# Holding the early loads of a fused linear-attention and SwiGLU kernel, and another split of its last output tile

## The chip, the core and the metric

The kernel runs on one core of a Trainium2 chip. The metric is the device time of one execution in microseconds (us). The core has a matrix engine (TensorE, in the profile PE, with PEld for its weight loads), a vector engine (VectorE, DVE), a scalar engine (ScalarE, ACT), a general engine (GpSimd, POOL) and a sequencer that issues DMAs (SyncE, SP). Each engine works through its own list of instructions in order, and waits on semaphores for the others.

## The reference

The input x has 2048 tokens of 640 numbers in bfloat16. It is normalised once, and two branches are added to it:

```python
xn = _layernorm(x)                                   # 2048 x 640
q, k, v = split(xn @ wqkv)                           # 32 heads of 20
pq, pk  = q @ w_phi, k @ w_phi                       # per head, 20 x 20
phi_q   = concat(softmax(pq), softmax(-pq))          # 40 features; phi_k alike
kv, z   = phi_k^T v, sum of phi_k over the tokens
A       = (phi_q kv / (phi_q z + 1e-6)) @ wo
B       = (silu(xn @ w1) * (xn @ w3)) @ w2           # inner width 1536
out     = x + A + B
```

## The kernel before

**A planner.** The kernel describes its work as operations with the memory that each reads and writes, and a list scheduler in `_Program.schedule` orders them at build time: it keeps a clock for each engine with assumed durations, and takes the ready operation that could start first, among near equals the one with the higher level (a due time turned round). Up to 175 us of its clock the width of "near equal" is drawn from a random generator started with `SEED`. `emit` then writes the order out for each engine with the semaphore waits that the dependencies need. A DMA that depends on another DMA makes SP wait for that one's landing. Nearly all instructions are recorded by two helpers, so PE's matmuls have the line L619, the other engines' L627, plain DMAs L689 and DMA transposes L693.

**Units on PE.** A unit is a chain of matmuls into one, two or four of the eight PSUM banks. Its name says what it computes:
- V4, K4: value and feature-mapped key projection of token tile 4 (16 tiles of 128 tokens), 10 matmuls of 320 columns each. K's weights are wk folded with w_phi (the "fold" units, which read the transposed wk or wq and write `Wkp` or `Wqp`). ScalarE takes the exponentials of K's result into `ekt`, VectorE sums them over each head (the TENSOR_REDUCE) and inverts the sum, GpSimd multiplies.
- M0.3: the MLP's gate and up product for block 0 (512 tokens) and chunk 3 of 12 of the inner width, 10 matmuls of 512 columns. ScalarE computes a tanh into `th`, VectorE two steps `t` and `hT`, and then the banks are free.
- Q0.1: the feature-mapped query of a block, 5 matmuls of 512 columns and two exponentials.
- kv_sum, kv_back: the sum over all tokens and its way back into the layout that the queries need.
- qt4: query times kv for tile 4, always in banks 4 to 7; ScalarE copies the denominators, VectorE divides and writes the product. The next qt can start when the product is written.
- O15: the output of tile 15, 12 chunks of hT by w2 and 5 of oT by wo, 640 columns in two banks; VectorE adds x, SP stores.

**Tokens and transposes.** x is loaded with tokens on the partitions (`x_tok`: tiles 0 to 3 one by one, tiles 4-7, 8-11 and 12-15 as loads of 640 KB). VectorE computes statistics, GpSimd the inverse deviation, VectorE or ScalarE normalises in place. Tiles 0 to 3 are transposed on PE; each tile from 4 on by one DMA transpose from SP (`turn`, here "turn 4" for tile 4) into `xnT`, which V, K, M and Q read.

**The early loads.** All go out on SP, but for four at the start on ScalarE's queue. Their order follows their levels. After x's first tiles, wv, the first third of w1 and w3 (480 KB each) and w_phi come the five transposes of wk. Then, in order of level: x tiles 4-7, w1 and w3 (second third, columns 384 to 768), x tiles 8-11, w1 and w3 (768 to 1152), x tiles 12-15, w1 and w3 (1152 to 1536), five transposes of wq. In the kernel before each of these waits for the last transpose of wk (`d.raw.add(o)`, in the list from `P.all[n]` on) and for nothing else, so SP issues them one after another.

**The last output tile.** O15 is computed in two halves of 320 columns, each with its own bank, addition and store, so that the first half's tail runs beside the second half's matmuls.

Of the kernel before, what the change touches and what calls it, by code (L numbers as in the profile page):

```python
# [5 lines left out]
ALU = mybir.AluOpType  # L6
# [4 lines left out]
D = 640  # L11
# [3 lines left out]
T = S // 128  # L15
# [477 lines left out]
CENTRED = {0: "ACT", 1: "ACT", 2: "ACT", 3: "DVE"}  # L493
POOLED = ()
TURNED = ()
SEED = 65
TRIPLES = ((0, 3, 0, 60), (3, 3, 60, 60), (6, 3, 120, 60), (9, 3, 180, 60), (12, 3, 240, 60), (13, 3, 300, 20))


def bass_parallel_sum__linear_kernel_hedgehog__glu_gated_swiglu__prompt_kernel(  # L500
# [13 lines left out]
    P = _Program(nc)  # L514
# [12 lines left out]
    def new(name, shape, dtype, offset=None):  # L527
        size = mybir.dt.size(dtype)
        for n in shape[1:]:
            size *= n  # L530
        return P.sbuf(name, shape, dtype, region(size) if offset is None else offset)
# [23 lines left out]
    xres = new("xres", [128, 4, D], bf)  # L555
# [42 lines left out]
    def bank(k, cols=512, off=0, p0=0, p1=128):  # L598
        return PS[p0:p1, k * 512 + off:k * 512 + off + cols]

    def bank2(k, cols):
        return PS[:, k * 512:(k + 2) * 512].rearrange("p (b c) -> p b c", c=512)[:, :, 0:cols]

    def free(ap):
        n = 1
        for s in ap.shape[1:]:
            n *= s
        return n
# [6 lines left out]
    def mm(j, o, l, r, start, stop, shared=False, busy=None):  # L615
        u, n = P.unit, free(r)

        def emit():
            return nc.tensor.matmul(o(u.k), l, r, start=start, stop=stop, skip_group_check=shared)  # L619
        return P.mm(emit, [l, r], j, max(n / 2400 + 0.0025, 0.035) if busy is None else busy, n)  # L620

    def way(eng, name, args, kw, busy, lat):
        u = P.unit
        e = {"ACT": nc.scalar, "DVE": nc.vector, "POOL": nc.gpsimd}[eng]

        def emit():
            return getattr(e, name)(*[at(a, u) for a in args], **{k: at(v, u) for k, v in kw.items()})  # L627
        emit.__name__ = name
        return eng, (emit, busy, lat)
# [5 lines left out]
    def sb(*aps):  # L635
        return [a for a in aps if hasattr(a, "ap")]

    def add(ways, w, r, banks=None, level=0.0, after=(), part=False):
        o = P.op(dict(ways), sb(*w), sb(*r), banks, level, after)
        o.part = part  # L640
        return o
# [11 lines left out]
    def w_tt(eng, o, a, b, f, n, fast=1):  # L653
        if eng == "DVE":
            return way(eng, "tensor_tensor", (o, a, b, f), {}, 0.07 + n / 960 / fast, 0.15 + n / 960 / fast)
        return way(eng, "tensor_tensor", (o, a, b, f), {}, 0.14 + n * 1.7 / 1000, 0.18 + n * 1.7 / 1000)
# [25 lines left out]
    def pieces(o, elem):  # L682
        n = 1
        for s in o.shape:
            n *= s
        return n * 2 / elem / 16, max(18.5, 12 + 0.04 * elem) / 1e3

    def load(o, i, level=0.0, eng="SP", after=()):
        return P.dma(eng, lambda: queue[eng].dma_start(o, i), sb(o), sb(i), *pieces(o, 2 * o.shape[-1]), 0.45, level,  # L689
                     after)  # L690

    def turn(o, i, level=0.0, dram=False, after=()):
        d = P.dma("SP", lambda: nc.sync.dma_start_transpose(o, i), sb(o), sb(i), *pieces(o, 256),  # L693
                  1.31, level, after)
        d.extra = 1.0 if dram else 0.2
        return d
# [4 lines left out]
    out_t = out.rearrange("b (t p) d -> p (b t) d", p=128)  # L701
# [5 lines left out]
    def load_x(a, b, level, eng="SP", after=()):  # L707
        return load(x_tok[:, a:b, :], x_t[:, a:b, :], level, eng, after)

    def load_w1(a, b, level, eng="SP"):  # L710
        return load(w1_s[:, :, a:b], w1_t[:, :, a:b], level, eng)

    def load_w3(a, b, level, eng="SP"):
        return load(w3_s[:, :, a:b], w3_t[:, :, a:b], level, eng)

    def load_w13(a, b, level, eng="SP"):
        load_w1(a, b, level, eng)
        load_w3(a, b, level, eng)

    def load_wT(which, e, level, after=()):  # L720
        return turn(wqkT[:, which * DC + e:which * DC + e + 1, :],
                    A_wqkv[:, which * D + 128 * e:which * D + 128 * e + 128], level, True, after)
# [42 lines left out]
    def ln_stats(t0, n, level):  # L765
        for t in range(t0, t0 + n):
            for q in range(2):
                i, o = x_tok[:, t, 320 * q:320 * q + 320], bst[:, t, 6 * q:6 * q + 6]
                add([w_op("DVE", "bn_stats", (o, i), 0.48, 0.5)], [o], [i], None, level)
            o, i = mv[:, t, 0:2], bst[:, t, 0:12]  # L770
            add([w_op("DVE", "bn_aggr", (o, i), 0.13, 0.21)], [o], [i], None, level)
        m, v, r, z = mv[:, t0:t0 + n, 0], mv[:, t0:t0 + n, 1], mv[:, t0:t0 + n, 4], mv[:, t0:t0 + n, 6]
        add([w_op("POOL", "tensor_scalar_add", (r, v, EPS), 0.21, 0.25)], [r], [v], None, level)
        add([w_op("POOL", "tensor_tensor", (r, r, mhalf[:, 0:n], ALU.pow), 0.55 + 0.1 * (n - 1),
                  0.6 + 0.1 * (n - 1))], [r], [r, mhalf[:, 0:n]], None, level)
        if t0 >= 4:
            add([w_op("POOL", "tensor_scalar_mul", (z, m, -1.0), 0.21, 0.25)], [z], [m], None, level)
            add([w_op("POOL", "tensor_tensor", (z, z, r, ALU.mult), 0.21, 0.25)], [z], [z, r], None, level)

    def ln_apply(t, level):  # L780
        o, m, s, z = x_tok[:, t, :], mv[:, t, 0:1], mv[:, t, 4:5], mv[:, t, 6:7]
        ways = [w_op("DVE", "tensor_scalar", (o, o, m, s, ALU.subtract, ALU.mult), 0.35, 0.44)]
        if t in POOLED:
            ways = [w_op("POOL", "tensor_scalar", (o, o, m, s, ALU.subtract, ALU.mult), 2.5, 2.55)]
        if t >= 4:
            ways.append(w_act(o, o, ACT.Identity, D, s, z))
        add(ways, [o], [o, m, s, z] if t >= 4 else [o, m, s], None, level)
# [274 lines left out]
    finish = []  # L1062

    def out_tile(t, level):
        b, ti = divmod(t, 4)
        u = P.begin(2, level, stream="O")
        u.name = f"O{t}"
        chunks = [(hT[b][:, i, ti * 128:(ti + 1) * 128], w2_s, i) for i in range(FC)]
        chunks += [(oT[:, i, t * 128:(t + 1) * 128], wo_s, i) for i in range(DC)]
        r = xres[:, t % 4, :].rearrange("p (b c) -> p b c", c=320)  # L1070
        load(xres[:, t % 4, :], x_t[:, t, :], 2e5 - 2 * t)
        if t < 4:
            P.all[-1].early = 60.0
        last = t == T - 1
        for qs in ([(0,), (1,)] if last else [(0, 1)]):
            for n, (l, w, i) in enumerate(chunks):
                for q in qs:
                    mm(q, lambda k, q=q: bank(k + q, 320), l, w[:, i, 320 * q:320 * q + 320], n == 0,
                       n == len(chunks) - 1)
            if last:  # L1080
                q = qs[0]
                add([w_tt("DVE", r[:, q, :], lambda k, q=q: bank(k + q, 320), r[:, q, :], ALU.add, 320)],
                    [r[:, q, :]], [r[:, q, :]], [q], 2e6)
                finish.append(load(out_t[:, t, 320 * q:320 * q + 320], r[:, q, :], 3e5))
            else:
                if qs[0] == 0:
                    add([w_tt("DVE", r, lambda k: bank2(k, 320), r, ALU.add, D)], [xres[:, t % 4, :]],
                        [xres[:, t % 4, :]], [0, 1], 1e6)
                    finish.append(load(out_t[:, t, :], xres[:, t % 4, :], 3e5 - 2 * t))

    def filler(t, until):
        u = P.begin(1, 0.0)
# [36 lines left out]
    for e in range(DC):  # L1129
        o = load_wT(1, e, lv - 9 - e, first)  # L1130
    load_x(4, 8, lv - 19, "SP", [o])
    n = len(P.all)
    load_w13(384, 768, lv - 20)
    load_x(8, 12, lv - 21)
    load_w13(768, 1152, lv - 22)
    load_x(12, 16, lv - 23)
    load_w13(1152, 1536, lv - 24)
    for e in range(DC):
        load_wT(0, e, lv - 30 - e)
    for d in P.all[n:]:  # L1140
        d.raw.add(o)

    up = 2e6
    for t in range(4):
# [2 lines left out]
    n = len(P.all)  # L1147
# [13 lines left out]
    for t in range(4, T, 2):  # L1161
        ln_stats(t, 2, 1e5 - t)
        ln_apply(t, 2e5 - t)
        ln_apply(t + 1, 2e5 - t)
        turn(xnT[:, :, t * 128:(t + 1) * 128], x_tok[:, t, :], lv)
        turn(xnT[:, :, t * 128 + 128:(t + 2) * 128], x_tok[:, t + 1, :], lv)

    def when(us):
        return 1000.0 - us
# [11 lines left out]
    n = len(P.all)  # L1181
# [8 lines left out]
    for b in range(3):  # L1190
        for fc in range(FC):
            n = 12 * b + fc
# [6 lines left out]
    for b in range(NB):  # L1199
        for j in range(4):  # L1200
            t = 4 * b + j
# [6 lines left out]

    P.schedule({"PE": 1.25, "ACT": 1.12, "DVE": 0.93, "POOL": 0.8, "SP": 0.81}, filler, 12.0, SEED, 175.0)

# [60 lines left out]
```

The softmax here doesn't subtract the row's maximum and nothing guards it: scores larger than these inputs give would overflow.

## Time and profile before

| | us |
|---|---|
| median of 4 runs | 276.12 (275.6 to 277.5) |
| the profiled execution | 277.5 |
| its span, first to last instruction | 275.7 |
| PE busy | 269.6 (98%) |
| VectorE busy | 183.6 (67%) |
| ScalarE busy | 102.7 (37%) |
| GpSimd busy | 60.4 (22%) |

The granted PE clock is 1.000. The runs are 277.5, 276.15, 275.6 and 276.1; the profiled execution is the first of them. Times inside the profile count from the span's start. In a timeline row the columns are the start, the length, the engine, the line, the operation with what it writes and reads, the count, and in brackets how long the engine stood idle before it and whose event came last before it went on. Merged rows count several instructions. A DMA row of the issues has size and the time from issue to landing. A "q" after an engine's name means its sequencer: the length of an SPq row is the time that issuing took.

### The profile page before, as it was taken

To read this page: it belongs to the slowest core of one execution; us is meant where nothing else is said; L and a number is where in the kernel's file an instruction comes from. 1 tells how busy PE (TensorE), PEld (TensorE's weight loads), DVE (VectorE), ACT (ScalarE), POOL (GpSimd) and SP (SyncE) were. 2 spreads that over 40 slices of the span, in tenths; PEclk is the share of its full clock that TensorE was granted. 3 is DMA by queue.
4 is the path that set the end of the run, shared out by engine and by line. 5 is a ranking of instruction groups with operands and counts; after the bars stand their busy time and mean duration, and the time that the engine had idled before them with its cause. 6 is when DMAs were issued, how large, how long until landed. Compare 5 with 4: busy or idle time off the path is not lost.

```text
span 275.7 us, 5081 instructions
## 1 busy us (share of the span) xinstructions
PE 269.6 (98%) x2104; PEld 159.8 (58%) x2104; DVE 183.6 (67%) x322; ACT 102.7 (37%) x188; POOL 60.4 (22%) x101
## 2 busy tenths in 40 slices
PE   8999979999999999999999999999999999999996
PEld 4747447765664446544444445777677774444774
DVE  5848886999999544478769986277677215566212
ACT  5637628874455441237383364010110002322000
POOL 4500633699989800000000000000000000000000
PEclk9999999999999999999999999999999999999999
DMA  7569998771000000802131111234343322000001
GB/s 234 153 95 283 342 158 174 121 207 57 0 0 2 0 0 2 270 18 26 24 50 21 27 26 25 72 95 85 98 110 80 90 71 74 0 0 0 26 24 48
DMA packets 41287, 21.98 MB, mean 80 GB/s; under 512 B 27056, under 2 KB 41264, under 8 KB 41264
## 3 DMA queue, kind: packets, MB, share of 16 engines
q1 hardware_dynamic: 40688, 21.01, 31.7%
q10 hardware_dynamic: 576, 0.66, 0.7%
q8 instruction: 16, 0.26, 0.4%
q14 instruction: 7, 0.06, 0.1%
HBM read 12.81 MB, written 2.62 MB: 56 GB/s over the span
## 4 chain that ended last, share of the span: by engine, by line
PE 93%; DMA 2%; DVE 2%; issue 1%; ACT 0%; ACTq 0%; DVEq 0%
PE PS L619 92%; DMA x_tok<-in_A_x_dram 2%; DVE bst L627 0%; PE PS L857 0%; DVE t L627 0%; DVE hT L627 0%; ACTq L689 0%; DVE Wqp L627 0%; ACT th L627 0%; ACT L627 0%; DVE xres L627 0%; DVE rS L627 0%; DVE xc L627 0%; DVE x_tok L627 0%; PE PS L1099 0%
## 5 line engine op out<-in xcount | busy, mean ns | idle before, releaser
L619 PE MATMUL PS<-xnT,w_s 128*128 128x512 bf16 x480 | 107.3, 379 | 0.0
L619 PEld LDWEIGHTS PS<-xnT,w_s 128*128 128x128 bf16 x480 | 46.4, 98 | 54.1 <-DVE hT L627 0.3
L619 PE MATMUL PS<-w_s,hT 128*128 128x320 bf16 x384 | 55.0, 299 | 0.0
L627 ACT ACTIVATE th<-PS 128x512 f32<-128x512 f32 x48 | 28.7, 598 | 64.0 <-PE PS L619 63.8
L627 DVE SCALAR_TENSOR_TENSOR t<-th,PS 128x512 bf16<-128x512 f32 x48 | 32.8, 683 | 26.4 <-ACT th L627 26.3
L619 PEld LDWEIGHTS PS<-w_s,hT 128*128 128x128 bf16 x384 | 37.0, 98 | 14.9
L627 POOL TENSOR_TENSOR ekt<-ekt,rS 128x640 bf16<-128x640 bf16 x32 | 39.6, 1276 | 1.9 <-DVE rS L627 1.9
L627 DVE TENSOR_TENSOR xres<-PS,xres 128x640 bf16<-128x640 f32 (+1 forms) x17 | 13.4, 785 | 39.0 <-PE PS L619 39.0
L627 DVE SCALAR_TENSOR_TENSOR hT<-t,PS 128x512 bf16<-128x512 bf16 x48 | 32.6, 678 | 1.3 <-DVE t L627 0.2
L627 ACT ACTIVATE EqT<-PS 128x512 bf16<-128x512 f32 x40 | 21.9, 594 | 12.0 <-PE PS L619 12.0
L627 ACT ACTIVATE e_s<-PS 128x64 f32<-128x64 f32 x32 | 9.1, 283 | 44.3 <-PE PS L619 43.9
L619 PE MATMUL PS<-wo_s,oT 128*128 128x320 bf16 x160 | 24.5, 299 | 0.0
L627 DVE TENSOR_TENSOR prod<-PS,g_s 128x1280 bf16<-128x1280 f32 x16 | 23.9, 1491 | 0.5
L619 PE MATMUL PS<-Wkp,xnT 128*128 128x320 bf16 x160 | 23.9, 299 | 0.0
L627 ACT ACTIVATE ekt<-PS 128x640 bf16<-128x640 f32 x32 | 20.8, 700 | 7.7 <-PE PS L619 7.5
L619 PE MATMUL PS<-xnT,Wqp 128*128 128x512 bf16 x100 | 23.4, 380 | 0.0
L627 DVE TENSOR_REDUCE S<-ekt 128x64 f32<-128x1280 bf16 x16 | 22.8, 1449 | 0.0
L619 PE MATMUL PS<-wv,xnT 128*128 128x320 bf16 x120 | 18.3, 299 | 1.7 <-DVE bst L627 1.7
L619 PEld LDWEIGHTS PS<-wo_s,oT 128*128 128x128 bf16 x160 | 15.7, 98 | 6.1
L619 PEld LDWEIGHTS PS<-Wkp,xnT 128*128 128x128 bf16 x160 | 15.5, 98 | 6.1 <-ACT Wkp L627 0.2
L627 DVE BATCH_NORM_STATS2 bst<-x_tok 128x6 f32<-128x320 bf16 x32 | 14.2, 471 | 3.8 <-DMA x_tok<-in_A_x_dram 3.8
L619 PEld LDWEIGHTS PS<-wv,xnT 128*128 128x128 bf16 x120 | 11.7, 98 | 7.3 <-DVE bst L627 2.2
(69 smaller groups left out, 168.1 us busy)
## 6 DMA issues: line engine op xcount, KB each, us to landing
w_s<-in_B_w_dram SPq DMA_DIRECT2D x8, 480.0 KB, 7.5
xres<-in_A_x_dram SPq DMA_DIRECT2D x16, 160.0 KB, 2.2
out_dram<-xres SPq DMA_DIRECT2D x15, 160.0 KB, 1.8
x_tok<-in_A_x_dram SPq DMA_DIRECT2D x3, 640.0 KB, 7.5
w_s<-in_B_w_dram SPq DMA_DIRECT2D x1, 1920.0 KB, 9.0
wo_s<-in_A_wo_dram SPq DMA_DIRECT2D x1, 800.0 KB, 5.6
x_tok<-in_A_x_dram SPq DMA_DIRECT2D x2, 160.0 KB, 3.6
x_tok<-in_A_x_dram ACTq DMA_DIRECT2D x2, 160.0 KB, 4.4
```

Source lines behind the costliest of these rows:

```text
L619: return nc.tensor.matmul(o(u.k), l, r, start=start, stop=stop, skip_group_check=shared)
L627: return getattr(e, name)(*[at(a, u) for a in args], **{k: at(v, u) for k, v in kw.items()})
```

## The change

Three things change.
- The list of loads that wait for the last transpose of wk is replaced by a chain: each load from the fourth on (counted from x tiles 4-7) waits for the landing of the third before it, so that at most three are on the way. x tiles 4-7 and the second third of w1 wait for the transpose of wk as before; the second third of w3, third in the list, waits for nothing now. x tiles 8-11 wait besides for `held`'s added dependency, the DMA transpose of tile 5 (which SP issues after that of tile 4).
- The last output tile is split into 384 and 256 columns.
- The planner's random generator starts from another number, so that the order of units, and of the work on all engines, differs in many places up to its 175 us, and behind.

```diff
-SEED = 65
+SEED = 136
...
-        last = t == T - 1
-        for qs in ([(0,), (1,)] if last else [(0, 1)]):
...
+        for q, c0, c1 in ((0, 0, 384), (1, 384, D)):
+            for n, (l, w, i) in enumerate(chunks):
+                mm(q, lambda k, q=q, c=c1 - c0: bank(k + q, c), l, w[:, i, c0:c1], n == 0, n == len(chunks) - 1)
+            o = xres[:, t % 4, c0:c1]
+            add([w_tt("DVE", o, lambda k, q=q, c=c1 - c0: bank(k + q, c), o, ALU.add, c1 - c0)], [o], [o], [q], 2e6)
+            finish.append(load(out_t[:, t, c0:c1], o, 3e5))
...
-    n = len(P.all)
+    n = len(P.all) - 1
     load_w13(384, 768, lv - 20)
     load_x(8, 12, lv - 21)
+    held = P.all[-1]
     load_w13(768, 1152, lv - 22)
     load_x(12, 16, lv - 23)
     load_w13(1152, 1536, lv - 24)
     for e in range(DC):
         load_wT(0, e, lv - 30 - e)
-    for d in P.all[n:]:
-        d.raw.add(o)
+    for m in range(n + 3, len(P.all)):
+        P.all[m].raw.add(P.all[m - 3])
+    P.all[n + 1].raw.add(o)
...
         turn(xnT[:, :, t * 128:(t + 1) * 128], x_tok[:, t, :], lv)
         turn(xnT[:, :, t * 128 + 128:(t + 2) * 128], x_tok[:, t + 1, :], lv)
+        if t == 4:
+            held.raw.add(P.all[-1])
```

In the order that the planner makes of the changed program, SP's list from w_phi on reads: w3 (384 to 768), five wk transposes, w3 (768 to 1152), x tiles 4-7, w1 (384 to 768), w3 (1152 to 1536), w1 (768 to 1152), one wq transpose, turns 4 and 5, w1 (1152 to 1536), turns 6 and 7, x tiles 8-11, a wq transpose, x tiles 12-15, two wq transposes, turns 8 to 11, the last wq transpose, turns 12 to 15. PE's list from the folds of wk on reads: K0 to K3, M0.3, M0.4, M0.5, V4, K4 and so on to K7, M0.6, M0.7, V8, K8 and so on to V12 with the folds of wq, where the kernel before has M0.6 ahead of V4 and M0.7 ahead of V12.

More of the change, by code (lines that the diff above doesn't have):

```diff
@@ L1073, in out_tile @@
             P.all[-1].early = 60.0
-        last = t == T - 1
-        for qs in ([(0,), (1,)] if last else [(0, 1)]):
+        if t < T - 1:
             for n, (l, w, i) in enumerate(chunks):
-                for q in qs:
+                for q in range(2):
                     mm(q, lambda k, q=q: bank(k + q, 320), l, w[:, i, 320 * q:320 * q + 320], n == 0,
                        n == len(chunks) - 1)
[L1080 to L1089, printed above, removed]
+            add([w_tt("DVE", r, lambda k: bank2(k, 320), r, ALU.add, D)], [xres[:, t % 4, :]],
+                [xres[:, t % 4, :]], [0, 1], 1e6)
+            finish.append(load(out_t[:, t, :], xres[:, t % 4, :], 3e5 - 2 * t))
+            return
+        for q, c0, c1 in ((0, 0, 384), (1, 384, D)):
[4 more added lines that the diff above has]
+            finish.append(load(out_t[:, t, c0:c1], o, 3e5))
     def filler(t, until):
```

## The prediction

> **What bounds the kernel now.** I read the page's busy shares and slices first, then TensorE's (PE's) timeline for its idle places, then the DMA landings around them.
>
> ```profile
> span 275.7 us, 5081 instructions
> PE 269.6 (98%) x2104; PEld 159.8 (58%) x2104; DVE 183.6 (67%) x322; ACT 102.7 (37%) x188; POOL 60.4 (22%) x101
> PE   8999979999999999999999999999999999999996
> ```
>
> PE works 98% of the span at full clock, in an order fixed when the program is built. The change does not alter PE's amount of work, so only PE's 6.1 us of idle time can be won. The sixth slice (a 7) is the one hole between start and end. PE's timeline gives its place:
>
> ```profile
> 28.36 8.80 PE L619 MATMUL PS<-xnT,w_s 128*128 128x512 bf16 x40
> 38.89 1.52 PE L619 MATMUL PS<-wv,xnT 128*128 128x320 bf16 x10 [1.74 <-DVE bst L627]
> 40.25 1.52 PE L619 MATMUL PS<-Wkp,xnT 128*128 128x320 bf16 x10
> 64.45 1.52 PE L619 MATMUL PS<-Wkp,xnT 128*128 128x320 bf16 x10
> 66.22 0.80 PE L619 MATMUL PS<-BDc,wqkT 128*128 128x140 bf16 x12 [0.25 <-DVE Wqp L627]
> ```
>
> Ten matmuls of 512 columns start 2.157 us before their successor (60.62 to 62.78), ten of 320 columns 1.358 (38.89 to 40.25 and on). So four MLP units (M0.3 to M0.6) from 28.36 would end at 36.99; V4, the value projection of token tile 4, starts at 38.89: 1.90 us lost. In the same way 64.45 + 1.36 = 65.81 against 66.22: 0.41 us lost at a fold of wq. Everything later stands nose to tail.
>
> The name in the first bracket is not the cause: the statistics that VectorE computes there are of tiles 8 on, and V4 does not read them. V4 needs the transpose of tile 4 (turn 4). From SP's timeline and the DMA issues, its issue and landing, and those of some loads before it:
>
> ```profile
> 28.86 3.06 SPq L693 DMA_TRANSPOSE xnT<-x_tok  x1
> xnT<-x_tok SPq DMA_TRANSPOSE x1, 9.9
> ...
> x_tok<-in_A_x_dram SPq DMA_DIRECT2D x1, 640.0 KB, 4.2
> ...
> w_s<-in_B_w_dram SPq DMA_DIRECT2D x1, 480.0 KB, 5.3
> ...
> w_s<-in_B_w_dram SPq DMA_DIRECT2D x1, 480.0 KB, 8.5
> ...
> xnT<-x_tok SPq DMA_TRANSPOSE x1, 2.7
> ```
>
> Turn 4 is issued at 28.86 and lands 9.9 us later, at 38.76; a transpose with nothing queued takes 2.7 (the last row, issued at 44.32). The difference is the queue: the loads issued from 20.28 land 4.2, 5.3, 6.3, 7.5, 8.5, 8.5, 10.3 and 10.1 us after their issue, that is at 24.5, 26.0, 27.6, 29.3, 30.9, 32.3, 35.7 and 37.0. Turn 4 stands behind all of them.
>
> **The change, part by part**, from the instruction order of the changed program.
>
> *What moves on SP.* The second third of w3 goes out at 4.3, ahead of the wk transposes, and the last-but-one w3 piece right behind them at 18.4. The DMA engines are idle from about 10 to 12.6 and from 19.7 to 21.3 in the trace; a 480 KB load takes 1.5 (32.3 - 30.9) to 1.6, so both fit. Both bounds for what they cost: nothing if they stay in the holes, or 0.3 us for the wk transposes (the last lands 20.2; the fold at 21.01 needs it by 21.28, 1.0 us of cover). I take nothing.
>
> Token tiles 4-7 go out at 20.28 as before and land at 24.5; w1's second piece lands at 26.0; the next w3 piece waits for a landing at 18.4 + 4.3 = 22.7 and takes third place, landing 27.5. Then come one w1 piece (issued 26.0) and one wq transpose (SP 27.5 to 28.8). Behind them are turns 4 and 5 at 28.86 (statistics and normalising on VectorE keep their order, ended 28.8 before) and 30.2. Ahead of turn 4 in the queue are then one w1 piece, sent by 28.1, and one transpose. Landing: 2.7 (alone) to 4.4 (a transpose from HBM, issued behind a load at 39.03), so 31.6 to 33.3.
>
> *What moves on PE.* M0.6 goes behind K7, so V4 is reached at 28.36 + 3 x 2.157 = 34.83. Turn 4 is there 1.5 to 3.2 earlier; turns 5, 6, 7 (issued 30.2, 33.3, 34.6, after 2.7 to 4.4) are needed at 37.55, 40.27 and 42.98 and have at least 2.5. V4's PSUM banks come from M0.4: on VectorE a sum over heads ends at 32.4 (31.0 + 1.4), then M0.3's hT, M0.4's t and hT follow at 0.6 to 0.7 each, so 34.3: 0.5 to spare. So the 1.90 us go; from V4 on every unit runs 1.90 earlier for the same work done.
>
> *The added waits.* SP stops for landings, and what stands behind is held too. Tiles 8-11 wait for turn 5, but SP comes to them only at 35.9 (after turns 6 and 7); landing 4.2 later, 40.1. Tiles 12-15 wait for that landing: 40.2 + 4.2 = 44.4. A wq transpose waits for it (44.4 to 45.7), and turns 8 to 11 stand behind at 45.7, 47.0, 48.3 and 49.6. Turn 8 lands at 48.4. PE needs it after eight projections (10.87) and two MLP units (4.31): 34.83 + 15.18 = 50.0. Cover 1.6 us. Turn 12, issued at 53.2 after its normalising, lands by 57.6, needed at 60.9. The remaining wq transposes are in by 55, folded from 62.3. So the waits cost nothing here, and the last loads could slip by 1.6 us.
>
> A rule speaks against holding. The Trainium skill, DMA: Bandwidth & Descriptors, section "Anatomy of one DMA", gives every DMA about 2.0 us of fixed cost (fitted on the GpSimd path) plus its bytes at 436 GB/s: by estimate 3.5 us for 640 KB, paid in full by every load that waits for another's landing, and its Rule under "Bandwidth" is to send more at once. With 3.5 turn 8 would land at 47.0, with the same forecast.
>
> The row says the same more dearly: 4.2 alone against 1.7 between landings in the full queue, 2.5 us lost for each of the two held x loads. The cover above already contains these.
>
> *The second idle place.* The wq folds are reordered; the VectorE copy that frees the banks has 0.3 us of cover by the rows (copy 0.74, reduce 1.4, reciprocal 0.46). VectorE had a 0.75 us gap without a visible cause at 63.0 there. Gain 0 to 0.41; I take 0.2.
>
> *The new order from 110 on.* Attention tiles qt4 and qt5 stand one MLP and one q unit apart: 0.49 + 1.08 + 2.16 + 0.12 = 3.85 us instead of 4.92. The bank of qt5 is free when qt4's product ends: seven exponentials first (0.54 each), then two copies and 1.13 of small VectorE operations and 1.41, about 3.94 after qt4's start. Then VectorE has 5.65 us of work (3.05 for a tile, 2.6 for two MLP units) in 4.92 us periods up to qt7, which is reached as its bank comes free. Cost 0.1 to 0.7; I take 0.1, nearest to the row of before, where the same load made no idle time.
>
> *The last tile.* 17 matmuls of 384 and 17 of 256 columns carry the columns of 34 of 320. The add at the end shrinks from 0.49 (320 columns) by 64/960 to 0.42; the output piece from 80 to 64 KB. Gain 0.1; bounds 0 and 0.15.
>
> Sum: -1.90 - 0.2 + 0.1 - 0.1 = -2.1; I keep 2.0. The span becomes 273.7 and the profiled execution 277.5 - 2.0 = 275.5. That execution lies 1.4 above the median of the runs, 276.12; taken from the median: **274.1 us**. A measurement here can tell about 0.5%, 1.4 us, from no change.
>
> **The rivals.**
> (1) *V4 still waits* (10%). If turn 4 lands as late as before (38.8), PE has reached it 2.16 earlier with one MLP unit less done and loses 4.06 instead of 1.90: 276.1 + 2.2 = 278.3, slower. It breaks even when turn 4 takes 7.8 us, and wins all from 5.9 down. For: SP issues it at the same 28.86. Against: of the eight loads ahead of it in the trace three go out later and two earlier, against one new (w3's last piece).
> (2) *The wait moves to V8* (10%). If the two held x loads take 6 us each (between the 4.2 and 7.5 rows), turn 8 lands 3.6 later and V8 waits 2.0: 276.1, nothing won; at 5 us no loss.
> (3) *The new order costs* (12%): 0.7 at qt5 to qt7 and the fold's gap stays: 275.1.
> (4) *The change does not reach the unprofiled runs* (10%): the profiled execution is 1.4 to 1.9 us above the other three, and most of the hole may belong to it alone. Then 0.8 is won: 275.3. Against: the queue's bytes are the same in every execution.
>
> **How the numbers follow.** The forecast has 58%: 273.4 (both gains whole) to 274.7. Cases (3) and (4) and half of (2) lie within 0.5% of 276.12, with a little of (3) below: faster 60%, same 25%, slower 15%. For 8 in 10 the range runs from 273.4 to 276.4; outside are (1) and the worse half of (2).
>
> **What would show it.** Right: V4 starts near 34.8 without idle time before it, turn 4's landing near 3 to 4 us, and PE's idle time in the sixth slice gone. V8 near 50.0, kv_sum at about 106.8, the last unit at about 266. Wrong: idle time before V4 or V8 with a transpose landing then, or gaps at qt5 to qt7; a start of the first fold after 21.3 would show the early w3 load in the way.

## The result, and the profile after

| | before | after |
|---|---|---|
| median, us | 276.63 (275.6 to 277.56, 78 runs) | 277.46 (275.71 to 279.3, 53 runs) |
| profiled execution, its span | 277.5, 275.7 | 277.76, 276.0 |

The ratio is 1.0031, with a 95% interval of 1.0022 to 1.004: the change made the kernel slower, by 0.8 us or 0.3%. The forecast was 274.1, with a range from 273.4 to 276.4. 276.63 is the median over all runs of the study; in those shown before it was 276.12.

The page of the changed kernel: the busy times, and PE's busy tenths in 40 slices of 6.9 us.

```profile
PE 269.8 (98%) x2104; PEld 158.9 (58%) x2104; DVE 183.0 (66%) x322; ACT 102.8 (37%) x188; POOL 61.1 (22%) x101
...
PE   8999999998999999999999999999999999999996
```

PE works as long as before. The 7 of the sixth slice is a 9, and the tenth slice (62 to 69 us) has become an 8: idle time went from one place and came back in another. PE's timeline shows both:

```profile
28.82 5.55 PE L619 MATMUL PS<-xnT,w_s 128*128 128x512 bf16 x25 [0.31 <-DMA w_s<-in_B_w_dram]
34.54 1.25 PE L619 MATMUL PS<-xnT,w_s 128*128 128x512 bf16 x5 [0.17 <-DVE hT L627]
36.16 1.52 PE L619 MATMUL PS<-wv,xnT 128*128 128x320 bf16 x10 [0.37 <-DMA xnT<-x_tok]
...
51.38 1.60 PE L619 MATMUL PS<-wv,xnT 128*128 128x320 bf16 x10
...
63.99 1.52 PE L619 MATMUL PS<-Wkp,xnT 128*128 128x320 bf16 x10
66.85 0.80 PE L619 MATMUL PS<-BDc,wqkT 128*128 128x140 bf16 x12 [1.33 <-DVE Wqp L627]
```

V4 starts at 36.16, where the forecast had 34.83: 1.33 us are lost in three pieces (waiting for w1's second piece at 28.82, for VectorE at 34.54, for turn 4 at 36.16). V8 stands at 51.38 and did not wait. The wq fold starts at 66.85, 2.86 us after K12 instead of 1.36: 1.50 lost, against 0.41 before. PE is idle in front of the folds because VectorE is late with the copy into `Wqp`.

The way to V4, from SP's timeline and the DMA issues (size, us to landing). The rows are: the third w3 piece, tiles 4-7, then three w pieces; the first wq transpose; turns 4 and 5.

```profile
18.75 0.58 SPq L689 DMA_DIRECT2D w_s<-in_B_w_dram  x1
20.57 0.37 SPq L689 DMA_DIRECT2D x_tok<-in_A_x_dram  x1
20.98 8.08 SPq L689 DMA_DIRECT2D w_s<-in_B_w_dram  x3
30.08 2.01 SPq L693 DMA_TRANSPOSE wqkT<-in_A_wqkv_dram  x1
32.13 2.60 SPq L693 DMA_TRANSPOSE xnT<-x_tok  x2
```

```profile
x_tok<-in_A_x_dram SPq DMA_DIRECT2D x1, 640.0 KB, 6.7
w_s<-in_B_w_dram SPq DMA_DIRECT2D x1, 480.0 KB, 7.7
...
xnT<-x_tok SPq DMA_TRANSPOSE x1, 3.9
```

VectorE's first statistics of tiles 4-7, which can start when these have landed:

```profile
27.29 0.89 DVE L627 BATCH_NORM_STATS2 bst<-x_tok 128x6 f32<-128x320 bf16 x2 [3.56 <-DMA x_tok<-in_A_x_dram]
```

Tiles 4-7, issued at 20.57, land 6.7 us later at 27.3, not at 24.5; w1's second piece, issued at 20.98, at 28.7, just before M0.3 starts. SP issues the wq transpose only at 30.08, since that waits for a w3 piece to land. Turn 4 goes out at 32.13 instead of 28.86, and lands 3.9 later, at 36.0.

V8's transpose, turn 8, heads a row of four on SP:

```profile
48.53 6.03 SPq L693 DMA_TRANSPOSE xnT<-x_tok  x4
xnT<-x_tok SPq DMA_TRANSPOSE x1, 2.7
```

It is issued at 48.53, where the forecast had 45.7, and lands 2.7 later, at 51.2: 0.15 before V8 starts.

### The profile page after: what moved, and what is told of

The parts are those of the page before. It is cut to its first block, busy times and chain, and to the rows that moved or that the text cites. A ratio compares the mean times of both kernels' runs of the same rounds, so it can differ in the third digit from the quotient of the medians.

```text
span 276.0 us, 5075 instructions
## 1 busy us (share of the span) xinstructions
PE 269.8 (98%) x2104; PEld 158.9 (58%) x2104; DVE 183.0 (66%) x322; ACT 102.8 (37%) x188; POOL 61.1 (22%) x101
## 4 chain that ended last, share of the span: by engine, by line
PE 75%; DVE 8%; DMA 8%; SPq 4%; POOL 2%; issue 1%; ACT 1%
PE PS L619 75%; DMA x_tok<-in_A_x_dram 4%; DMA phi_s<-in_A_w_phi_dram 3%; SPq L693 3%; DVE bst L627 2%; DVE S L627 2%; POOL mv L627 2%; DVE x_tok L627 2%; DMA wqkT<-in_A_wqkv_dram 1%; SPq L689 1%; DVE rS L627 1%; ACT x_tok L627 1%; DVE mv L627 0%; DVE t L627 0%; DVE hT L627 0%
## 5 line engine op out<-in xcount | busy, mean ns | idle before, releaser
L627 ACT ACTIVATE th<-PS 128x512 f32<-128x512 f32 x48 | 28.7, 597 | 71.9 <-PE PS L619 71.6
L619 PE MATMUL PS<-w_s,hT 128*128 128x320 bf16 (+2 forms) x384 | 55.0, 299 | 0.0
L627 DVE TENSOR_TENSOR xres<-PS,xres 128x640 bf16<-128x640 f32 (+2 forms) x17 | 13.4, 785 | 40.0 <-PE PS L619 40.0
L619 PE MATMUL PS<-wo_s,oT 128*128 128x320 bf16 (+2 forms) x160 | 24.5, 299 | 0.0
L619 PEld LDWEIGHTS PS<-xnT,Wqp 128*128 128x128 bf16 x100 | 9.4, 98 | 11.0
```

## The experiments

All runs compare with the kernel before on the same chip. Where an edit moves instructions, it is made in the finished plan, so every engine that is not named keeps its order to the last instruction. `move(a, b, to)` puts entries a to b of SP's list ahead of entry `to`; `reorder` puts the listed entries in the order given. w1 and w3 come in four pieces of 384 columns, called by their first column: 0, 384 (the second), 768 (the third), 1152 (the last).

**c_split: the tail alone, and a second profile of before.**

```diff
-        for qs in ([(0,), (1,)] if last else [(0, 1)]):
+        for q, c0, c1 in ((0, 0, 384), (1, 384, D)):      # last tile only, as in the change
```

> The kernel before with nothing but the last tile's split of 384 and 256; all engines keep the order of before. Forecast's term for the tail: 0.1 us less (0 to 0.15), so 276.5 against 276.6, a ratio of 0.9996. Rival: the tail has grown (in the changed kernel the second half's last matmul stands about 0.3 us later against the last tile's start than before), then 0.2 to 0.4 more, 1.001. It also gives a second profile of everything before the last tile: the forecast took the idle time before V4 as 1.90 us in every execution; if it belongs to that one execution, V4 stands at 37.0 to 38 here, with under 1.2 us of idle time.

276.69, ratio 1.0005 (0.9991 to 1.0018). From the end of the last matmul to the span's end 2.54 us pass, in c_held, with the old split, 2.60: the term is 0.06 and can't be seen in the times. V4, whose transpose (turn 4) is issued at 28.95 and lands 9.4 later, at 38.4:

```profile
28.53 8.58 PE L619 MATMUL PS<-xnT,w_s 128*128 128x512 bf16 x39
38.49 1.52 PE L619 MATMUL PS<-wv,xnT 128*128 128x320 bf16 x10 [1.39 <-DVE hT L627]
```

39 of 40 matmuls are recorded, so M0.3 began one spacing earlier, at 28.32, and V4 was due at 28.32 + 8.63 = 36.95: a hole of 1.54 us, up to turn 4's landing. The 1.90 of the forecast was partly one execution's.

**c_held: only the loads behind turn 4 are held, in the order of before.** Tiles 12-15 and w1's last piece (the expectation calls it the third) go behind turn 7; no wait is added.

```diff
+    move(18, 19, 24)
```

> The kernel before, with the loads of token tiles 12-15 and of the third w1 piece moved behind the DMA transposes of tiles 4 to 7 on SP, all other orders as before, no wait added: the holding alone. Theory (the queue ahead of turn 4 makes the hole, the change held the wrong loads): turn 4 is issued at about 28.9, lands by 34.5 to 36, V4 starts at 37.0 and 1.0 to 1.9 us go: 274.7 to 275.6, ratio 0.993 to 0.996. Rival (the hole is small in ordinary executions, or turn 4 is slow whatever is queued ahead): 276.3 to 276.6, ratio 0.999 to 1.000, with the transpose of tile 4 still landing over 8 us after its issue.

275.33, ratio 0.9951 (0.9932 to 0.997). SP's timeline, the issue of turn 4 and PE:

```profile
29.01 6.02 SPq L693 DMA_TRANSPOSE xnT<-x_tok  x4
```

```profile
xnT<-x_tok SPq DMA_TRANSPOSE x1, 5.1
```

```profile
28.61 8.58 PE L619 MATMUL PS<-xnT,w_s 128*128 128x512 bf16 x39
37.03 1.52 PE L619 MATMUL PS<-wv,xnT 128*128 128x320 bf16 x10
```

Turn 4 lands 5.1 us after its issue (9.4 in c_split), and V4 follows without idle time. 275.33 is where the theory had it, and the mechanism of the forecast is shown: the loads queued ahead of turn 4 make the hole, and holding two of them is worth 1.4 us.

**x_turns: in the changed kernel, tiles 4-7 and w1 (384) ahead of w3 (768), and turns 4 and 5 ahead of the loads that wait for landings.**

```diff
+    move(14, 15, 13)
+    move(16, 18, 21)
```

> The changed kernel, with two moves on SP alone: x tiles 4-7 and the second third of w1 ahead of the third w3 piece, and turns 4 and 5 ahead of the loads that wait for landings and of the first wq transpose. All waits of the chain are kept. Order theory (x tiles 4-7 are late because a w3 piece went ahead, and turn 4 because SP stood waiting for another w3 piece): tiles 4-7 land near 24.5 and not 27.3, turn 4 is issued at 28.9 and lands by 32 to 33, V4 starts at 34.8 to 35.0 instead of 36.16: 1.2 us less, 276.2 to 276.4. The hole at the fold of wq, 1.5 us, stays at first sight, perhaps smaller by the three us by which VectorE starts earlier. Limit theory (three loads on the way are too few to fill the queue): tiles 4-7 still need over 6 us, V4 stays near 36: 277.3 to 277.6.

281.41, ratio 1.0165 (1.0137 to 1.0192): far from both expectations, and yet the order theory held up to V5. VectorE's, SP's and PE's timelines:

```profile
24.78 0.89 DVE L627 BATCH_NORM_STATS2 bst<-x_tok 128x6 f32<-128x320 bf16 x2 [1.18 <-DMA x_tok<-in_A_x_dram]
```

```profile
28.99 2.55 SPq L693 DMA_TRANSPOSE xnT<-x_tok  x2
31.59 1.15 SPq L689 DMA_DIRECT2D w_s<-in_B_w_dram  x2
35.92 1.26 SPq L693 DMA_TRANSPOSE wqkT<-in_A_wqkv_dram  x1
37.36 0.45 SPq L689 DMA_DIRECT2D w_s<-in_B_w_dram  x1
37.86 2.54 SPq L693 DMA_TRANSPOSE xnT<-x_tok  x2
```

```profile
42.96 2.82 PE L619 MATMUL PS<-wv,xnT 128*128 128x320 bf16 x10 [2.67 <-DMA xnT<-x_tok]
45.58 1.92 PE L619 MATMUL PS<-Wkp,xnT 128*128 128x320 bf16 x10
```

Tiles 4-7 land at 24.78, turn 4 is issued at 28.99, V4 starts at 34.70. But SP then stands until 35.92 for a w3 piece and until 37.36 for a w1 piece, and turn 6, which needs neither, goes out at 37.86. V6 waits 2.67 us for it, and the next matmuls run at half speed (below). A landing wait on SP holds whatever stands behind it.

**no_limit: the changed kernel and its order, without the landing waits.** Tiles 8-11's wait for turn 5 stayed; they stand behind it anyway.

```diff
+    for a, b in limit:              # the pairs of the chain
+        a.raw.discard(b)
```

> The changed kernel, every engine's order kept, SP's too, but without the waits of the loads and wq transposes for the landing of the third before (tiles 8-11 no longer wait for turn 5 in words, but still stand behind it on SP). Order theory (the third w3 piece ahead of tiles 4-7 makes these late): tiles 4-7 still land at 26.5 to 27.5, turn 4 is still issued near 31.5 and, with more loads ahead of it, lands at 36 to 38: V4 as late as in the changed kernel or later, 277.4 to 279. Limit theory (the waits themselves, SP standing still and a queue too short, cost the time): tiles 4-7 land before 25.5, V4 starts before 35.5, 276.0 to 276.5.

277.05, ratio 1.0016 (0.9999 to 1.0033). VectorE's first statistics of tiles 4-7, and M0.3:

```profile
28.02 0.89 DVE L627 BATCH_NORM_STATS2 bst<-x_tok 128x6 f32<-128x320 bf16 x2 [4.36 <-DMA x_tok<-in_A_x_dram]
```

```profile
29.84 6.69 PE L619 MATMUL PS<-xnT,w_s 128*128 128x512 bf16 x29 [1.40 <-ACT ekt L627]
```

Without the limit tiles 4-7 land at 28.0, a little later still, and PE stands 1.40 us before M0.3 (its w1 piece, issued at 20.99 behind the same load, lands 8.5 later, at 29.5; the releaser named there had long been done). So it is the order, w3 (768) ahead of tiles 4-7, and not the waits, that makes tiles 4-7 late.

**fold_copy: the changed kernel, VectorE's first `Wqp` copy ahead of a reduce and a reciprocal.**

```diff
...
+    i = P.ops.index(dve[105]) + 1   # the copy
+    P.ops[i:i] = dve[103:105]       # reduce and reciprocal, taken out before
```

> The changed kernel, with one move on VectorE: the copy that frees the bank of the first wq fold goes ahead of a reduce and a reciprocal (1.34 and 0.45 us) that nothing on TensorE waits for soon. Theory (VectorE is late there, since the statistics and the normalising of tiles 8 to 15 came late, and the copy in its line holds TensorE): the fold starts at 65.4 instead of 66.85, 1.4 us go: 276.0 to 276.2, ratio to the kernel before 0.998. Rival (the next copy or the MLP unit behind is as late, so the hole moves on): 276.9 to 277.4.

278.34, ratio 1.0067 (1.0043 to 1.0091). The hole left 66.85 and came back, 1.19 us long, at a later fold (PE's timeline):

```profile
73.16 0.49 PE L619 MATMUL PS<-BDc,wqkT 128*128 128x140 bf16 x6 [1.19 <-DVE Wqp L627]
```

The rival was right: VectorE has more work due there than time. Its median is 0.9 above the changed kernel's; its profile also has 0.92 us idle before M0.3 (the changed kernel's has 0.31) and 0.33 before V8, whose transpose landed late, where nothing was edited. Why these grew is open.

**held_right: the changed kernel with all its waits, SP's list put right.** Tiles 4-7 and w1 (384) ahead of w3 (768), turns 4 to 7 ahead of everything that waits, turns 8 to 11 ahead of the last wq transposes.

```diff
+    reorder((14, 15, 13, 19, 20, 22, 23, 24, 16, 17, 26, 21, 18, 29, 30, 31, 32, 25, 27, 28))
```

> The changed kernel with all its waits, and another order on SP alone: tiles 4-7 and w1's second third ahead of the third w3 piece, then turns 4 to 7, then tiles 8-11 and the loads that wait for landings, turns 8 to 11 ahead of the last wq transposes. Order theory: V4 near 34.8 and V6 near 40.2 without idle time; tiles 8-11 land near 39 instead of 43.0 and 12-15 near 43.5, so VectorE is some 4 us earlier with their statistics and the hole at the wq fold falls from 1.5 to under 0.7: 274.6 to 275.6. Limit theory: something still stands at a landing wait, V8 or a fold, by 1 us or more: 276.2 to 277.5.

276.27, ratio 0.9991 (0.9968 to 1.0014): 1.2 us better than the changed kernel, short of the expectation. No idle time before V4 or V6, but V12 starts 0.9 us late and the fold another 0.4: together again over 1 us. V12's transpose, turn 12, could go at 54, when its tile is normalised, but stands on SP behind four wq transposes, two of which wait 3.1 us together for earlier ones to land. It is issued at 59.30 and lands 2.6 later; V12 starts at 62.07.

**queue_136: the same without the landing waits** (and without tiles 8-11's wait for turn 5), and with w1 (768), w3 (1152) and tiles 8-11 ahead of turn 4, tiles 12-15 and w1 (1152) behind turn 7, as c_held has it.

```diff
+    for a, b in limit:
+        a.raw.discard(b)
...
+    reorder((14, 15, 13, 17, 16, 24, 19, 20, 22, 23, 26, 21, 18, 25, 27, 28))
```

> The changed kernel without the landing waits, SP in the order of the kernel c_held (tiles 4-7, the second thirds, tiles 8-11, the third w1 and w3 pieces but for w3's, which is out by then, turns 4 to 7, and only then tiles 12-15, w1's last piece and the wq transposes); the order of all other engines as in the changed kernel. VectorE theory (the fold hole is VectorE's backlog from late statistics): with tiles 8-11 landing near 30 the backlog is gone, V4 near 34.8 to 35.3, fold hole under 0.4: 274.6 to 275.3, as c_held. Rival (the changed order of units itself costs, at the folds and from qt4 on, 0.5 or more): 275.8 to 276.3.

276.10, ratio 0.9981 (0.9966 to 0.9996). V4 without idle time, at 34.95; but PE at the fold, and VectorE and GpSimd before it:

```profile
62.67 1.52 PE L619 MATMUL PS<-Wkp,xnT 128*128 128x320 bf16 x10
65.31 0.80 PE L619 MATMUL PS<-BDc,wqkT 128*128 128x140 bf16 x12 [1.12 <-DVE Wqp L627]
```

```profile
53.00 0.80 DVE L627 TENSOR_SCALAR x_tok<-x_tok,mv 128x640 bf16<-128x640 bf16 x2 [0.34 <-POOL mv L627]
...
56.45 2.68 DVE L627 TENSOR_SCALAR x_tok<-x_tok,mv 128x640 bf16<-128x640 bf16 x2
```

```profile
56.37 10.03 POOL L627 TENSOR_TENSOR ekt<-ekt,rS 128x640 bf16<-128x640 bf16 x8
```

Tiles 8-11 were there early, and the hole stayed (2.64 us from K12 to the fold, 1.28 too many): my theory that late statistics make VectorE's backlog falls. The rows show another: two normalisings of a tile (`x_tok` from `x_tok` and `mv`) take 0.80 us at 53.00 and 2.68 at 56.45, when GpSimd runs product after product of 1.25 us. The changed kernel has the same pair (2.68 at 57.99, products from 57.90 on). In the kernel before, one of the two is caught:

```profile
52.98 1.72 DVE L627 TENSOR_SCALAR x_tok<-x_tok,mv 128x640 bf16<-128x640 bf16 x2
52.89 1.27 POOL L627 TENSOR_TENSOR ekt<-ekt,rS 128x640 bf16<-128x640 bf16 x1
```

**norm_act: queue_136, and ScalarE normalises tiles 14 and 15.** **after_act: the same edit in the changed kernel, nothing else.**

```diff
...
+    for o in dve[97:99]:
+        o.eng, o.emit = "ACT", o.ways["ACT"][0]
```

> queue_136 with one edit: ScalarE instead of VectorE normalises token tiles 14 and 15. In queue_136 these two took VectorE 2.68 us beside GpSimd's products of ekt (1.25 to 1.27 us each), where two without a product beside them take 0.80; the copy of the wq fold came 1.1 us late. Theory (these blocked normalisings are VectorE's backlog): the copy comes 2.7 us earlier in VectorE's order, the fold's hole of 1.12 goes, 276.10 - 1.1 = 275.0. Rival (VectorE is behind for other reasons, or ScalarE, which copies and exponentiates for V and K, holds TensorE instead): 275.7 to 276.4.

> The changed kernel with the same single edit, ScalarE instead of VectorE for the normalising of tiles 14 and 15, the loads as changed. Theory: of the 1.5 us at the fold 1.1 to 1.5 go, the 1.33 us up to V4 stay: 276.0 to 276.4, equal to or slightly faster than the kernel before. Rival (late statistics of tiles 8 to 15 keep VectorE behind even so): the hole shrinks by less than 0.6, 276.9 to 277.4.

norm_act has 274.54, ratio 0.993 (0.9917 to 0.9944), and the fold follows K12 without a gap:

```profile
62.51 1.52 PE L619 MATMUL PS<-Wkp,xnT 128*128 128x320 bf16 x10
63.87 0.79 PE L619 MATMUL PS<-BDc,wqkT 128*128 128x140 bf16 x12
```

after_act has 276.04, ratio 0.9978 (0.9956 to 0.9999), 1.4 below the changed kernel, with no idle time at the fold and 1.0 us still lost before V4 (35.84). So these two normalisings on VectorE make the fold's hole. That it is their slowing and not their mere place is worked out, not run: at 0.80 for the pair, as at 53.00, VectorE would be 1.88 us earlier, more than either hole (1.28 and 1.50).

**seed_only** and **holds_only: each part of the change without the other.** The edit shown is seed_only's, in the kernel before; holds_only is the changed kernel with 65 for 136.

```diff
-SEED = 65
+SEED = 136
```

> The kernel before with the planner started from 136 and nothing else changed (the planner then places units itself: V4 behind M0.5 instead of M0.6, an MLP unit after K10). Turn 4 stands behind the same eight loads and lands near 38.5, V4 is reached at 34.8: 3.7 us idle instead of 1.4: 278.5 to 279.5 if nothing else changes. Rival (the new order makes it up later): 276.5 to 277.5.

> The changed kernel with the planner started from 65: the holding and the split without the other start. SP's order up to turn 7 comes out the same as in the changed kernel, so tiles 4-7 land near 27.3 and turn 4 near 36; the planner puts V4 behind M0.4, reached at 32.7 to 33.2: 2.9 to 3.4 us idle. 278 to 279 if the fold costs as before (0.3), more if VectorE is behind there. Rival (the early w3 piece does not delay tiles 4-7 by itself): V4 without idle time, 275.5.

seed_only has 280.83, ratio 1.0138 (1.0111 to 1.0164). It issues turn 4 at 29.71, which lands 8.5 later, and V4 waits 2.89 us:

```profile
38.37 1.52 PE L619 MATMUL PS<-wv,xnT 128*128 128x320 bf16 x10 [2.89 <-DVE bst L627]
```

The profiled execution took 279.33, 1.5 us less than the median. Its granted clock is 1.000, as is that of the other execution below 280 (278.92); the four from 280.71 to 281.15 have a mean clock of 0.994, as x_turns has in all five of its executions (0.993 to 0.994). So the difference goes with a stretch of lower clock, as in x_turns; where it lies in these four no trace shows. holds_only has 276.84, ratio 1.0017 (1.0002 to 1.0033). I had expected 278 to 279: V4 started at 34.90 instead of near 36 (turn 4, issued at 31.60, took at most 3.3 us), and there was no gap at the fold. PE still waited 1.16 us for V4 and 0.28 within it. So the new start needs the holding, and the two together cost 0.3%.

**c_best: c_held with the split, and with the copy of the first fold ahead of a reciprocal and an MLP product on VectorE.**

```diff
+    move(18, 19, 24)
...
+    P.ops[i:i] = dve[103:105]       # behind the copy, as in fold_copy
```

> c_held with the last tile's split and with VectorE's copy of the first wq fold ahead of a reciprocal and an MLP product. c_held had 275.33, with 0.27 us idle at the fold and a tail of 2.6 us behind the last matmul; the split had 2.54. Sum 275.33 - 0.27 - 0.06 = 275.0, ratio to the kernel before 0.994. Rival (the fold's gap moves on to the next fold or to the MLP unit): 275.3.

274.69, ratio 0.9923 (0.9896 to 0.9951). The fold's gap is gone here, since VectorE has no backlog behind it. c_best and norm_act, two different orders, end at the same time and beat both kernels, by 1.9 us and more: after the start no idle time of note is left on PE in either.

## Why the prediction was wrong

1. **The hole at V4: the mechanism was right, its size too large.** c_held shows turn 4 behind the queue, worth 1.4 us, not 1.90. The fourth rival (the hole is smaller outside the profiled execution) was right by 0.4 to 0.5 us, not by the 1.1 that it had. The forecast took the hole from the slowest of four executions and subtracted it from their median.

2. **The step that failed first: "so both fit", "I take nothing", tiles 4-7 "land at 24.5".** I costed the third w3 piece as a load that fills an idle stretch of the queue. But it is issued 1.8 us ahead of tiles 4-7, and these stood behind it: 6.7 us instead of 4.2. The forecast itself had that piece land at 22.7, after tiles 4-7 go out, and still kept the 4.2 of the row before. The 1.5 us for 480 KB were the distance of two landings in a full queue; this piece took 4.3 from issue to landing, as the next paragraph of the forecast has it. w1's second piece came late with it, at 28.7 instead of 26.0, so M0.3 waited. Busy times by window (PE, PEld, VectorE, ScalarE, GpSimd; then the granted clock, the DMA share and GB/s), before and then after:

```profile
22.00:24.00 2.00, 1.96 (x22) 1.38 (x20) 1.73 (x3) 1.46 (x3) 0.00 (x0) 1.00 0.95 333
24.00:26.00 2.00, 2.00 (x17) 1.45 (x15) 1.46 (x5) 1.46 (x3) 0.00 (x0) 1.00 1.10 339
```

```profile
22.00:24.00 2.00, 1.96 (x22) 1.37 (x20) 1.72 (x3) 1.44 (x3) 0.00 (x0) 1.00 0.85 222
24.00:26.00 2.00, 2.00 (x17) 1.47 (x15) 0.00 (x0) 1.47 (x3) 0.00 (x0) 1.00 0.96 285
```

The queue also moved less at that time than in the kernel before, 222 and 285 GB/s against 333 and 339. From 24 to 26 it moved 287 in no_limit, which has the order without the waits, and 345 in x_turns, which has the waits without the order; so this goes with the order too, and why is open. That the order causes the lateness is shown by x_turns and queue_136 (tiles 4-7 at 24.8 and 25.0) against no_limit (28.0). VectorE stood idle for 3.56 us, and everything hung on that landing: statistics, normalising, turn 4. The first rival (V4 still waits) named the right place, with turn 4 late from being issued late rather than from its queue. V4 lost 1.33, so of the 1.54 us of c_split 0.2 were won.

3. **The second step that failed: "SP 27.5 to 28.8" for the wq transpose.** I took the landing of w3 (1152) as 27.5; SP stood until 30.08. In the changed kernel tile 4 was normalised only by 31.4, so this cost 0.7 us at most; x_turns, where tiles 4-7 are on time and the landing waits stand ahead of turn 6, shows the price: 2.67 us at V6.

4. **The wq fold: sized at 0.2 us of gain, it was a loss of 1.09** (1.50 against 0.41). "0.3 us of cover" was summed from the copy, a reduce and a reciprocal at the durations of before. The two normalisings further ahead on VectorE were not in that sum at all; the new order puts both beside GpSimd's products, where they take 1.34 each instead of 0.40. What a moved instruction runs beside was missing from the working. The third rival ("the fold's gap stays") had the place.

5. **V8 did not wait, but by luck.** The forecast had 1.6 us of cover: turn 8 issued at 45.7, landing at 48.4, V8 due at 50.0. SP came to tiles 8-11 at 37.99 instead of 35.9, and the held loads took 5.0 and 4.3 us; turn 8 landed at 51.2. V8 stood at 51.38 = 36.16 + 15.18 + 0.04, just behind it, because V4 was late as well; at the forecast's 50.0 it would have waited 1.2. In fold_copy V8 waited 0.33. The second rival named this place.

6. **qt4 to qt5 and the tail were right**: 3.91 us from qt4 to qt5 against 3.85, so 0.06 of cost where 0.1 was taken, and 0.06 of gain at the end where 0.1 was.

The sum against c_split's profile, the more ordinary one of before's order: -0.2 at V4 (1.33 for 1.54), +1.1 at the fold, +0.1 at qt5, makes +1.0; its span is 275.0, that of after 276.0.

## What to carry to other kernels

Here a load put into an idle stretch ahead of a load that someone waits for delayed that load by some 3 us; ask what is issued next, not whether the stretch is free. SP issues in order, and in x_turns and held_right a wait for a landing held transposes that did not need it, so put the instructions that are due ahead of those that wait, and hold loads by their place in the list where that is enough (c_held adds no wait at all). When an order changes, price each moved vector instruction by what the other engines do at its new time, not by its mean.

## What the hardware showed that I had not expected

**VectorE's normalising beside GpSimd.** A normalising of 128x640 in bfloat16 takes 0.4 us alone and up to 1.39 while a GpSimd product (1.25 to 1.27 us) runs; reduces (1.42) and copies from PSUM (0.76 to 0.82) are as long beside products as without. The changed kernel:

```profile
54.55 0.80 DVE L627 TENSOR_SCALAR x_tok<-x_tok,mv 128x640 bf16<-128x640 bf16 x2 [0.34 <-POOL mv L627]
57.99 2.68 DVE L627 TENSOR_SCALAR x_tok<-x_tok,mv 128x640 bf16<-128x640 bf16 x2
```

```profile
57.90 5.12 POOL L627 TENSOR_TENSOR ekt<-ekt,rS 128x640 bf16<-128x640 bf16 x4
```

The Trainium skill, SBUF — State Buffer, section "Who interferes with whom", says that VectorE and GpSimd contend for one shared pair of ports, as an exclusive lock. The trace agrees in that each normalising lasts about as long as a product; the rule and the pair at 52.98 of the kernel before would have pointed to a loss at the fold, not a gain.

**PE's clock after a pause.** In x_turns PE stood for 2.67 us, and the granted clock (the third number from the end) fell to half for some 3.4 us:

```profile
42.00:43.00 1.00, 0.04 (x1) 0.07 (x2) 0.00 (x0) 0.00 (x0) 0.00 (x0) 0.98 1.24 306
43.00:44.00 1.00, 1.00 (x5) 0.53 (x6) 0.00 (x0) 0.00 (x0) 0.00 (x0) 0.50 1.10 334
...
46.00:47.00 1.00, 1.00 (x8) 0.61 (x6) 0.97 (x4) 0.53 (x1) 0.00 (x0) 0.81 0.57 38
```

V6 and K6 took 4.38 us (42.96 to 47.34) instead of 2.72, so the pause cost 1.7 us besides itself. All five executions of x_turns have a mean clock of 0.993 to 0.994. In seed_only's profile a pause of 2.89 us left the clock at 1.00, but four of its six executions have 0.994. The Trainium skill, TensorE: Matmul & The Clock Gate, section "What's actually happening", puts the return to half clock after an idle window of about 3.4 us that runs freely; here 2.67 us was enough in the profile of x_turns, and 2.89 was not in that of seed_only.
